# Layer 1's first product in the standard form, weight tile by weight tile over resident tokens

## The chip, the cores and the metric

The program runs on one core of one Trainium2 chip. The core has engines that work side by side, each through its own list of instructions in order: TensorE (PE, matmuls and their weight loads, PEld), VectorE (DVE), ScalarE (ACT) and GpSimd (POOL); SyncE (SP) issues most of the transfers, and ACT and POOL issue some. Instructions wait for one another through semaphores. Data lie in SBUF (128 partitions), matmul results in PSUM, the rest in the chip's memory (DRAM here). The metric is the device time in microseconds (us) of one execution; lower is better.

## The reference

Attention with a bias from relative positions, then two layers of the same kind: a matrix product to 2048 features, an elementwise activation, and a product back to 512. What matters of it:

```python
# q, k, v: (4, 8, 576, 64); x after attention: 2304 tokens x 512
scores = scale * np.matmul(q, k.transpose(0, 1, 3, 2))
scores = scores + bias.transpose(2, 0, 1)[None, :, :, :]
attn = softmax(scores)              # exp(scores - max) / (sum + 1e-09)
x = (attn @ v) as (2304, 512)
h = x @ w_in0                       # layer 0: 512 x 2048
x = (h * np.cos(h)) @ w_out0        # 2048 x 512
h = x @ w_in1                       # layer 1
g = np.maximum(h, 0.0) + alpha * np.minimum(h, 0.0)   # alpha: one number per feature
out = g @ w_out1
```

The inputs come as 64-bit floats. The kernel makes 32-bit floats of them on the chip.

## The kernel before

**Numbers.** Every 64-bit weight tile of 128 x 512 (a *raw*, 512 KB) is read as two 32-bit halves and put together: `conv`, lines 195 to 226, with two ACT steps (L204, L205), two DVE steps (L208 or, with a change of sign, L210; then L212) and a POOL addition (L215). A matmul runs on numbers of reduced precision, so each operand is kept as a rounded part *hi* and a remainder *lo* (`split_to`: ACT makes hi at L234, POOL or DVE the lo at L236), and a product is three matmuls: hi·hi, hi·lo and lo·hi.

**Stages**, one after the other on PE:
1. *Attention*: 16 pairs of heads. Beside it runs a list of background jobs (`JOBS`): the weights of layer 0's first product (`wi0`, 16 tiles; the first `NDIR` = 8 stay in SBUF, the others go to DRAM and come back), and the output weights of layer 0 (`stage_wo(0, k)`, k from 4 to 7; there are 8 sets in all, each from two raws).
2. *Layer 0, first product* (`h_phase0`): 5 token tiles (three of 464, two of 456) x 16 weight tiles x 12 matmuls, standard form (L755). x is fetched and split (L741, L743) for each token tile. The activation h·cos h is ACT L764, DVE L765 and L766, ACT L768, DVE L769, and a write to DRAM (L770). In the background: `stage_wo(0, 0..3)`, kept in SBUF, then sets of layer 1 (`stage_wo(1, k)`, written to DRAM as `w2_d`).
3. *Layer 0, output product* (`o_phase(0)`): a Strassen-Winograd form, 7 products for each of 3 token groups s, 48 matmuls of 384 columns each (L952). The order of the products is `ORD` = 1, 5, 6, 3, 7, 2, 4. Operands (`op`) are fetched, combined (L892) and split (ACT L934, DVE L935). The weight sets `W1[p]` are loaded by SP while the stage begins.
4. *Layer 1, first product* (`h_phase1`): also Strassen-Winograd, 7 products x 8 chunks j x 3 token groups, each 6 matmuls of 384 columns (L1093). `x_prep` makes the combinations of x for each token group (L1065, L234, L236). `chunk_wi1(j)` makes a chunk of weights from two raws with a change of sign by `fl`, which is read from an extra input `alphab` (L298, L300), four sums (L308 to L312) and a split of seven slices (L314 to L316). The activation takes one ACT and one DVE step for each result (L1101, L1102) and a write (L1103).
5. *Layer 1, output product* (`o_phase(1)`): as stage 3, 7 x 3 products, each 72 matmuls of 256 columns. All seven sets of weights are loaded from `w2_d`, 1 MB at a time, two loads a set.

**What sets the order.** Each engine's list of instructions is laid out when the program is built, by a scheduler that places them by the time it reckons for each; the background jobs are generators that the main loops advance by a quota per step (`step`, WR = 2.4 in stage 3). Transfers through `fetch` (L176) go through SP's queue in the order of its list; before, POOL's queue carries ten loads in stage 2 and the writes of L253.

## Time and profile before

| what | us |
|---|---|
| median of 2 runs (lowest, highest) | 1236.49 (1234.80, 1238.19) |
| the profiled execution | 1240.88 |
| its span in the profile | 1238.9 |
| PE busy | 1088.2 (88% of the span), 7120 matmuls |
| PE weight loads busy | 934.3 (75%) |
| DVE busy | 919.1 (74%) |
| ACT busy | 685.2 (55%) |
| POOL busy | 392.0 (32%) |

The profile gives, for each instruction, its start and length on its engine. A *stretch* is a window of time with the busy time of each engine in it. A *timeline* row is a run of like instructions: its start, the length from the first's start to the last's end, and in brackets the idle time before it with what ended that. A *group* adds up the like instructions of a window. Matmuls overlap, so the time of one is the distance between starts and not its own length. The granted clock is the share of TensorE's full clock.

### The profile page before, as it was taken

How to read it: one execution, taken by the hardware profiler on the slowest of the kernel's cores; microseconds unless marked ns; L12 is line 12 of the kernel's file. 1: busy time of each engine (PE TensorE's matmuls, PEld its weight loads, DVE VectorE, ACT ScalarE, POOL GpSimd, SP SyncE). 2: the span in 40 equal slices, each digit the busy share in tenths (PEclk: the TensorE clock that was granted, in tenths of full speed). 3: DMA queues.
4: the chain of work that ended last, by engine and by line, in shares of the span. 5: the costliest groups of instructions: out<-in, count | busy, mean ns of one | idle time of the engine just before them, and what ended most of it. 6: DMA issues, size and time to landing. Idle time of an engine off the chain costs nothing. (4 is left out here: it accounts for less than half of the span.)

```text
span 1238.9 us, 19848 instructions
## 1 busy us (share of the span) xinstructions
PE 1088.2 (88%) x7120; PEld 934.3 (75%) x7120; DVE 919.1 (74%) x1552; ACT 685.2 (55%) x1241; POOL 392.0 (32%) x368
## 2 busy tenths in 40 slices
PE   7598989999878889999699999527999997799998
PEld 2245666666557778899699999527898997799998
DVE  8585777777766999999776767697688644658573
ACT  7595677666765767666544444433455432344442
POOL 6305576554446545433210000362354200000000
PEclk9698999999998999999799999858999998799999
DMA  7566547465457557666858253423365239963631
GB/s 231 185 184 194 180 129 255 168 200 171 157 174 280 175 179 236 221 211 232 306 185 280 64 191 107 162 72 102 128 216 183 106 134 408 347 190 118 211 96 52
DMA packets 117778, 229.80 MB, mean 185 GB/s; under 512 B 13488, under 2 KB 82096, under 8 KB 114992
## 3 DMA queue, kind: packets, MB, share of 16 engines
...
q0 software_dynamic: 5776, 19.93, 4.4%
...
## 5 line engine op out<-in xcount | busy, mean ns | idle before, releaser
L755 PE MATMUL h<-xhi,w 128*128 128x464 f32 (+1 forms) x640 | 191.7, 380 | 17.0 <-DVE tb L769 10.8
L755 PEld LDWEIGHTS h<-xhi,w 128*128 128x128 f32 x640 | 123.2, 193 | 34.4 <-DVE tb L769 13.1
L934 ACT ACTIVATE op<-a 128x768 fp32r<-128x768 f32 x84 | 70.8, 847 | 98.1 <-PE ob L952 26.0
L485 ACT ACTIVATE P<-P,nm 128x576 f32<-128x576 f32 x128 | 98.4, 770 | 47.4 <-DVE nm L472 47.1
L935 DVE TENSOR_TENSOR op<-a,op 128x768 fp32r<-128x768 f32 x84 | 79.5, 956 | 60.2 <-ACT op L934 58.6
L755 PE MATMUL h<-xlo,w 128*128 128x464 f32 (+1 forms) x320 | 120.9, 378 | 0.0
L472 DVE CUSTOM_DVE_ANT_0 P<-S,bt 128x576 f32<-128x576 f32 x128 | 91.8, 751 | 34.0 <-PE S L456 24.5
L215 POOL TENSOR_TENSOR wc<-wc,wp 128x512 int32<-128x512 int32 x64 | 87.4, 1366 | 87.6 <-DVE wc L212 58.3
L934 ACT ACTIVATE op<-b 128x768 fp32r<-128x768 f32 x84 | 70.3, 844 | 71.6 <-PE ob L952 22.5
L935 DVE TENSOR_TENSOR op<-b,op 128x768 fp32r<-128x768 f32 x84 | 80.7, 973 | 33.5 <-ACT op L934 33.5
L1093 PE MATMUL B<-x_t,ch 128*128 128x384 f32 x432 | 88.1, 348 | 10.7 <-DVE g L1158 6.6
L1093 PEld LDWEIGHTS B<-x_t,ch 128*128 128x128 f32 x432 | 78.1, 195 | 15.4 <-DVE g L1158 9.0
L952 PE MATMUL ob<-op,wo 128*128 128x384 f32 x432 | 79.0, 342 | 2.3 <-DVE op L935 2.3
L952 PEld LDWEIGHTS ob<-op,wo 128*128 128x128 f32 x432 | 77.3, 191 | 2.7 <-DVE op L935 2.6
L952 PE MATMUL ob<-wo,op 128*128 128x256 f32 x648 | 78.1, 281 | 0.0
L952 PEld LDWEIGHTS ob<-wo,op 128*128 128x128 f32 x648 | 77.3, 188 | 0.0
L1093 PE MATMUL A<-x_b,ch 128*128 128x384 f32 x288 | 58.7, 351 | 20.6 <-ACT ch L234 11.9
L768 ACT ACTIVATE tb<-tb,hpi 128x464 f32<-128x464 f32 (+1 forms) x80 | 54.1, 677 | 35.0 <-DVE tb L766 34.5
L456 PE MATMUL S<-kh,qh 64*128 64x288 f32 (+1 forms) x288 | 57.1, 352 | 16.4 <-DVE nm L472 16.4
L1093 PEld LDWEIGHTS A<-x_b,ch 128*128 128x128 f32 x288 | 53.0, 198 | 22.9 <-ACT ch L234 12.7
L766 DVE SCALAR_TENSOR_TENSOR tb<-ta,tb 128x464 f32<-128x464 int32 (+1 forms) x80 | 68.5, 859 | 0.7
L952 PE MATMUL oc<-wo,op 128*128 128x256 f32 x432 | 56.5, 293 | 12.4 <-ACT op L934 8.9
...
## 6 DMA issues: line engine op xcount, KB each, us to landing
...
raw<-in_wi_dram SPq DMA_DIRECT2D x32, 512.0 KB, 4.1
raw<-in_wo_dram SPq DMA_DIRECT2D x32, 512.0 KB, 3.9
...
```

The lines of the kernel that those rows point to most:

```text
L215: ge.tensor_tensor(out=c, in0=c, in1=p, op=ALU.add)
L456: te.matmul(ps[:, hf, 0:HS], lhsT=w[r, 128 * i:128 * i + 128], rhs=m[r, c0:c0 + HS], start=(j == 0), stop=(j == 2))
L472: keep(2, ve.tensor_tensor_reduce(out=sn.rearrange("p (a b) -> p a b", a=2), in0=ps[:, :, 0:HS], in1=bt[hp, s].rearrange("p (a b) -> p a b ...
L485: keep(3, se.activation(out=e, in_=e, func=AF.Exp, bias=nm, scale=-1.0, accum_out=sums[n, u][:, col, 0:1]))
L755: te.matmul(ps[:, 0:n], lhsT=w_[:, wx, w], rhs=xx[:, 0:n], start=(j == 0), stop=(j == 11))
L766: ve.scalar_tensor_tensor(out=g, in0=tt, scalar=-C2, in1=g, op0=ALU.mult, op1=ALU.add)
L768: se.activation(out=g, in_=g, func=AF.Sin, bias=hpi)
L934: se.activation(out=o[:, 0], in_=x, func=AF.Copy)
L935: ve.tensor_tensor(out=o[:, 1], in0=x, in1=o[:, 0].bitcast(F32), op=ALU.subtract)
L952: ins = te.matmul(ps[:, m], lhsT=x[:, sl] if L else w[:, sl], rhs=w if L else x, start=first, stop=kk == NK - 1 and n == 2, skip_group_che ...
L1093: ins = te.matmul(ps, lhsT=w[:, wl, sl, 128 * ks:128 * ks + 128], rhs=x[:, xl, ks], start=first and n == 0, stop=n == 5, skip_group_check= ...
```

## The change

Layer 1's first product is now in the standard form. All six token tiles of 384 (`X[q, i]`, hi and lo only) lie in SBUF, and the program goes weight tile by weight tile (f = 0 to 15) over the six: 16 x 6 x 12 = 1152 matmuls of 384 columns instead of 1008. A weight tile `v` comes from one raw (`wi(1, f)`), with hi from ACT and lo from DVE, and there are four buffers for them. The activation is one ACT step (scaled by the sign) and one DVE step (`act2`), and 96 writes to DRAM as before. `alphab`, its loads and the chunk's sums and slices are gone.

The output weights of layer 1 are all made in the background of this stage, k = 0 to 7 with the weight tiles between them. Products 1, 5, 6, 2 and 3 are combined straight into SBUF (`WO[1, g]`, tiles `wq`), and only 7 and 4 pass through DRAM (tiles `wp`). In `o_phase(0)` nothing runs in the background any more.

In layer 0 two sets more (k = 2, 3) are made during attention and only k = 0, 1 in stage 2; `NDIR` is 6; the first x tile is split during attention (pool `xh0`); remainders in `split_to` and those of later x tiles are made on DVE from stage 2 on; and ten weight loads stand on SP's queue instead of POOL's.

The diff, cut to its core:

```diff
-FIRST, SIDE, SMOD, BFIRST, BRATE, SPL, WS0, WSR, PER = 4, 6, 2, 8, 1.75, 3, 30, 3.8, 1.0
+FIRST, SIDE, SMOD, BFIRST, BRATE, SPL, WS0, WSR, PER = 4, 6, 2, 8, 1.75, 3, 28, 3.2, 1.0
...
-NDIR = 8
+NDIR = 6
 XA, HX = 6, 300
 RING, LO = 4, 3
-NW1, WR = 7, 2.4
+NIP, H0R, H1R = 2, 1.0, 3.2
 ORD = (1, 5, 6, 3, 7, 2, 4)
-GRP = ((1,), (5, 6), (3, 7), (2, 4))
+GRPS = (((1,), (5, 6), (3, 7), (2, 4)), ((1,), (5, 6), (2, 3), (7, 4)))
...
+    def leave_w(layer, k, g, x):
+        ps = GRPS[layer][g]
+        n = len(ps)
+        if (layer == 0 and k < NIP) or (layer == 1 and g < 3):
+            w = WO[layer, g]
+            yield from split_to(w[:, :, k, 0, :], w[:, :, k, 1, :], x)
             return
-        st = wpool["t"].tile([128, 2, 2, 256], F32R, tag="st", name=f"sw{layer}_{k}_{places[0][0]}")
...
+        st = wpool["t"].tile([128, 2, 2, 256], F32R, tag="st", name=f"sw{layer}_{k}_{g}")
...
+            order = (cols(u1, 1), ct[:, 0:2], cols(box[1], 2), ct[:, 2:4])
+        for g, x in enumerate(order):
+            yield from leave_w(layer, k, g, x)
-    def chunk_wi1(j):
...
+    def wi(layer, f):
         box = []
-        fl = wpool["f"].tile([128, 256], F32, tag="fl", name=f"fl{j}")
...
+        yield from conv(layer, f, 0, box)
+        if layer:
+            t = wt[f] = wpool["h"].tile([128, 2, 512], F32R, tag="w", name=f"v{f}")
+        elif f < NDIR:
             t = wt[f] = wpool["a"].tile([128, 2, 512], F32R, tag="w", name=f"w{f}")
         else:
             t = wpool["t"].tile([128, 2, 2, 256], F32R, tag="st", name=f"st{f}").rearrange("p a b c -> p a (b c)")
         hi, lo = t[:, 0], t[:, 1]
-        if HIA == 2:
+        if layer:
+            se.activation(out=hi, in_=box[0], func=AF.Copy)
+        elif HIA == 2:
             keep(0, ge.tensor_copy(out=hi, in_=box[0]))
         else:
             keep(0, se.activation(out=hi, in_=box[0], func=AF.Copy))
         yield
-        keep(1, (ge if LOP else ve).tensor_tensor(out=lo, in0=box[0], in1=hi.bitcast(F32), op=ALU.subtract))
+        keep(1, (ve if layer else ge).tensor_tensor(out=lo, in0=box[0], in1=hi.bitcast(F32), op=ALU.subtract))
...
-    JOBS += [(stage_wo, (0, k), 3.0, [(0, 2 * k, 1), (0, 2 * k + 1, 1)]) for k in range(4, NK)]
+    JOBS = [(wi, (0, f), 1.0, [(0, f, 0)]) for f in range(NF)]
+    JOBS += [(stage_wo, (0, k), 3.0, [(0, 2 * k, 1), (0, 2 * k + 1, 1)]) for k in range(NIP, NK)]
...
+                        wpool["x"] = astack.enter_context(tc.tile_pool(name="xh0", bufs=NCC, **right))
...
-                eng = ve if t == 0 and cc % 2 else ge
+                eng = ve if t else ge
...
-                ge.dma_start(out=wt[f], in_=w_d[f])
-            bg.extend(stage_wo(0, k) for k in range(4))
+                fetch(wt[f].bitcast(F32), w_d[f])
+            for g, ps in enumerate(GRPS[0]):
+                for i, p in enumerate(ps):
+                    fetch(WO[0, g][:, i, NIP:4].bitcast(F32), w2_d[0][SLOT[p], :, NIP:4])
+                    if p == 1:
+                        fetch(W1[1].bitcast(F32), w2_d[0][SLOT[1], :, 4:8])
+            bg.extend(stage_wo(0, k) for k in range(NIP))
...
-                quota += 1.6
+                quota += H0R
...
+                due = {(0, 5 if p == 7 else 6, 2 * h): [(W1[p][:, 4 * h:4 * h + 4], 4 * h)] for p in (7, 4) for h in range(2)}
+                weight = lambda p, k, x: W1[p][:, k, x] if p in (4, 7) else WO[1, PLACES[1][p][0]][:, PLACES[1][p][1], k, x]
...
-                bg.extend(stage_wo(1, k) for k in range(NW1))
...
     def h_phase1():
...
+        tiles = [(q, i) for q in range(NS3) for i in range(2)]
...
+            def x_prep(q):
+                x = {i: xs[q].tile([128, 2, NCC, TS], F32R, tag=f"x{i}", name=f"x{q}_{i}") for i in range(2)}
+                for i in range(2):
+                    fetch(x[i][:, 1].bitcast(F32), x1_d[q][:, :, i].rearrange("c p n -> p c n"))
                 yield
-
...
+                for i in range(2):
+                    for h in (slice(0, 2), slice(2, 4)):
+                        yield from split_to(x[i][:, 0, h], x[i][:, 1, h], x[i][:, 1, h].bitcast(F32))
+                    X[q, i] = x[i]
...
-                first = [x_prep(0), chunk_wi1(0), chunk_wi1(1)]
+                first = [x_prep(0), wi(1, 0), x_prep(1), wi(1, 1), wi(1, 2)]
...
+            ph = tile_pool(c, "ph", bufs=6, space=PSUM)
+            bg.append(x_prep(2))
+            nw = 3
+            for k in range(NK):
+                for _ in range(2):
+                    if nw < NF:
+                        bg.append(wi(1, nw))
+                        nw += 1
+                bg.append(stage_wo(1, k))
...
+                for cc in range(NCC):
+                    for wx, xx in ((0, 0), (0, 1), (1, 0)):
+                        ins = te.matmul(ps, lhsT=w[:, wx, 128 * cc:128 * cc + 128], rhs=x[:, xx, cc], start=(n == 0), stop=(n == 11))
...
+            def act2(f, q, i, ps):
+                g = gp.tile([128, TS], F32, tag="g", name=f"u{f}_{q}_{i}")
+                se.activation(out=g, in_=ps, func=AF.Copy, scale=sgn[:, f:f + 1])
+                ve.scalar_tensor_tensor(out=g, in0=ps, scalar=asg[:, f:f + 1], in1=g, op0=ALU.mult, op1=ALU.max)
+                t0 = TS * q + NH * i
+                se.dma_start(out=g_d[1][f, :, t0:t0 + TS], in_=g)
+            quota = 0.0
+            late = None
+            for f in range(NF):
+                for q, i in tiles:
+                    while (q, i) not in X or f not in wt:
+                        step()
+                    ps = emit_h(f, q, i)
+                    if late:
+                        act2(*late)
+                    late = (f, q, i, ps)
+                    quota += H1R
+                    step(int(quota))
+                    quota -= int(quota)
+            act2(*late)
```

The rows below show how the lists of the engines change at three places. In the names, `x1_0` is an x tile (group 1, half 0), `raw1_3_0` the raw of layer 1's weight tile 3, `wc` and `wp` the two halves of a raw in conversion, `v` a weight tile of layer 1, `op2_4_0` an operand of product 4 of token group 2, `o2_4` the last result of layer 0.

**ACT's list where layer 1's first product begins.** Before, from the first operand of layer 0's last product:

```order
L934 ACTIVATE op2_4_0_8483<-b11_2_0_7899 128x768
L934 ACTIVATE op2_4_1_8499<-b11_2_1_7920 128x768
L934 ACTIVATE op2_4_2_8515<-b11_2_2_7943 128x768
L985 ACTIVATE o2_2_8530<-oa2_8061 128x768
L934 ACTIVATE op2_4_3_8534<-b11_2_3_7968 128x768
L960 DMA x1_d2_61<-o2_2_8530 128x2x384
L234 ACTIVATE x_b11_0_8614<-x_b11_0_8614 128x768
L234 ACTIVATE x_b21_0_8615<-x_b21_0_8615 128x768
```

After, from the same operand:

```order
L895 ACTIVATE op2_4_0_8233<-b11_2_0_7748 128x768
L232 ACTIVATE x1_0_8388<-x1_0_8388 128x768 x2
L895 ACTIVATE op2_4_1_8249<-b11_2_1_7766 128x768
L232 ACTIVATE x1_1_8389<-x1_1_8389 128x768 x2
L895 ACTIVATE op2_4_2_8265<-b11_2_2_7784 128x768
L946 ACTIVATE o2_2_8280<-oa2_7878 128x768
L895 ACTIVATE op2_4_3_8284<-b11_2_3_7805 128x768
L921 DMA x1_d2_61<-o2_2_8280 128x2x384
```

Before, from the eviction of the last result (`o2_4`):

```order
L988 ACTIVATE o2_4_8585<-ob2_8140 128x768
L234 ACTIVATE x_b22_0_8616<-x_b22_0_8616 128x768
L960 DMA x1_d2_61<-o2_4_8585 128x2x384
L234 ACTIVATE x_b11_1_8603<-x_b11_1_8603 128x768
L234 ACTIVATE x_t1_0_8617<-xt1_0_8661 128x768
L234 ACTIVATE x_b21_1_8604<-x_b21_1_8604 128x768
L234 ACTIVATE x_t3_0_8618<-xt3_0_8678 128x768
L234 ACTIVATE x_b22_1_8605<-x_b22_1_8605 128x768
L234 ACTIVATE x_t2_0_8619<-xt2_0_8682 128x768
L205 ACTIVATE wp1_1_0_8685<-raw1_1_0_8680 128x512
L234 ACTIVATE ch0_8701<-wc1_0_0_8669 128x512
```

After, up to that eviction and behind it:

```order
L293 ACTIVATE v1_8409<-wc1_1_0_8399 128x512
L206 ACTIVATE wc1_3_0_8525<-raw1_3_0_8523 128x512
L207 ACTIVATE wp1_3_0_8526<-raw1_3_0_8523 128x512
L206 ACTIVATE wc1_2_0_8415<-raw1_2_0_8413 128x512
L206 ACTIVATE wc1_4_0_8571<-raw1_4_0_8569 128x512
L949 ACTIVATE o2_4_8335<-ob2_7945 128x768
L207 ACTIVATE wp1_4_0_8572<-raw1_4_0_8569 128x512
L921 DMA x1_d2_61<-o2_4_8335 128x2x384
L232 ACTIVATE x0_0_8365<-x0_0_8365 128x768 x2
L293 ACTIVATE v2_8422<-wc1_2_0_8415 128x512
L293 ACTIVATE v3_8549<-wc1_3_0_8525 128x512
L232 ACTIVATE x0_1_8366<-x0_1_8366 128x768 x2
```

The splits of six x combinations and a chunk's slices that followed the eviction are gone. Two splits of x tile 1 now stand among the operands of the last product, the hi parts of weight tiles 0 and 1 ahead of the eviction, and one conversion and the splits of x0 behind it.

**SP's list where layer 1's output product begins.** Before (`wo1_p` is half a weight set, `a11_0_0` and the like are parts of the activations):

```order
L176 DMA wo1_1_10660<-w2_d1_78 128x2048
L176 DMA a11_0_0_10711<-g_d1_80 128x2x384
L176 DMA a11_0_1_10713<-g_d1_80 128x2x384
L176 DMA wo1_1_10660<-w2_d1_78 128x2048
L176 DMA a11_0_2_10716<-g_d1_80 128x2x384
L176 DMA a11_0_3_10718<-g_d1_80 128x2x384
L176 DMA wo1_5_10653<-w2_d1_78 128x2048
L176 DMA a22_0_0_10724<-g_d1_80 128x2x384
L176 DMA a21_0_0_10726<-g_d1_80 128x2x384
L176 DMA a22_0_1_10731<-g_d1_80 128x2x384
L176 DMA a21_0_1_10733<-g_d1_80 128x2x384
L176 DMA wo1_5_10653<-w2_d1_78 128x2048
```

After:

```order
L178 DMA a11_0_0_10561<-g_d1_82 128x2x384
L178 DMA a11_0_1_10563<-g_d1_82 128x2x384
L178 DMA a11_0_2_10565<-g_d1_82 128x2x384
L178 DMA a11_0_3_10567<-g_d1_82 128x2x384
L178 DMA wp7_10549<-w2_d1_80 128x2048
L178 DMA a22_0_0_10573<-g_d1_82 128x2x384
L178 DMA a21_0_0_10575<-g_d1_82 128x2x384
L178 DMA a22_0_1_10580<-g_d1_82 128x2x384
L178 DMA a21_0_1_10582<-g_d1_82 128x2x384
L178 DMA wp7_10549<-w2_d1_80 128x2048
L178 DMA a22_0_2_10588<-g_d1_82 128x2x384
L178 DMA a21_0_2_10590<-g_d1_82 128x2x384
```

Of the loads of weight sets, three stood ahead of the eighth load of activations before; now one does, and the four activations of the first product come first.

**PE's list where layer 0's first product begins.** Before:

```order
L755 MATMUL h0_0_4898<-xhi0_0_4870,w0_1666 128x464
L755 MATMUL h0_1_4918<-xhi0_0_4870,w1_1734 128x464
L755 MATMUL h0_2_4945<-xhi0_0_4870,w2_1825 128x464
L755 MATMUL h0_3_4967<-xhi0_0_4870,w3_1961 128x464
L755 MATMUL h0_4_4994<-xhi0_0_4870,w4_2061 128x464
L755 MATMUL h0_5_5018<-xhi0_0_4870,w5_2151 128x464
L755 MATMUL h0_0_4898<-xlo0_0_4862,w0_1666 128x464
L755 MATMUL h0_0_4898<-xhi0_0_4870,w0_1666 128x464
L755 MATMUL h0_0_4898<-xhi0_1_4873,w0_1666 128x464
```

After:

```order
L725 MATMUL h0_0_5002<-xhi0_0_4962,w0_1588 128x464
L725 MATMUL h0_0_5002<-xlo0_0_4954,w0_1588 128x464
L725 MATMUL h0_0_5002<-xhi0_0_4962,w0_1588 128x464
L725 MATMUL h0_0_5002<-xhi0_1_4965,w0_1588 128x464
L725 MATMUL h0_0_5002<-xlo0_1_4956,w0_1588 128x464
L725 MATMUL h0_0_5002<-xhi0_1_4965,w0_1588 128x464
L725 MATMUL h0_0_5002<-xhi0_2_4968,w0_1588 128x464
L725 MATMUL h0_0_5002<-xlo0_2_4958,w0_1588 128x464
```

Before, six weight tiles' first matmuls on one x part stood ahead of the rest; after, the twelve matmuls of weight tile 0 stand in a row.

## Rows read from the trace of the kernel before

**Rows 1.** stretches: length, busy us of each engine, granted clock, DMA share, GB/s
```profile
0.00:375.00 375.00, 321.10 (x2633) 202.86 (x2633) 270.23 (x677) 258.46 (x574) 182.62 (x192) 0.96 0.60 188
375.00:390.00 15.00, 15.00 (x60) 12.93 (x61) 7.86 (x9) 7.82 (x14) 9.24 (x8) 0.83 1.07 389
390.00:594.00 204.00, 193.16 (x903) 171.32 (x902) 195.21 (x315) 140.77 (x240) 93.94 (x92) 0.98 0.59 201
594.00:790.00 196.00, 182.71 (x1009) 180.52 (x1007) 136.55 (x163) 90.00 (x116) 15.57 (x19) 0.96 0.55 182
...
801.00:825.00 24.00, 4.17 (x11) 2.73 (x10) 24.00 (x20) 9.75 (x14) 17.38 (x9) 0.50 0.38 123
825.00:900.00 75.00, 59.07 (x300) 56.46 (x300) 56.80 (x74) 32.01 (x60) 28.90 (x18) 0.87 0.31 104
900.00:1000.00 100.00, 94.22 (x519) 90.68 (x518) 75.75 (x123) 48.17 (x96) 37.80 (x32) 0.98 0.51 166
...
1037.00:1239.00 202.00, 184.80 (x1515) 183.70 (x1513) 125.29 (x139) 80.39 (x98) 0.00 (x0) 0.96 0.56 188
```

**Rows 2.** the same view, 20 us of attention and of layer 0's first product
```profile
240.00:260.00 20.00, 19.61 (x161) 13.17 (x162) 15.49 (x37) 12.75 (x31) 11.01 (x13) 1.00 0.55 186
...
430.00:450.00 20.00, 14.05 (x60) 11.77 (x59) 19.93 (x29) 13.45 (x25) 11.77 (x10) 0.91 0.59 208
```

**Rows 3.** PE's timeline, layer 0's first product: start, length, operation, [idle before]
```profile
374.92 2.69 PE L755 MATMUL h<-xhi,w 128*128 128x464 f32 x6 [6.18 <-ACT xhi L741]
...
395.90 0.59 PE L755 MATMUL h<-xhi,w 128*128 128x464 f32 x2
...
402.88 0.58 PE L755 MATMUL h<-xhi,w 128*128 128x464 f32 x2
```

**Rows 4.** PE's waits from 375 to 594: who waits for whom, us, times, longest
```profile
PE h L755 <- DVE tb L769: 10.8, 5, 4.2
```

**Rows 5.** PE's timeline, output product of layer 0
```profile
610.43 0.69 PE L952 MATMUL oc<-op,wo 128*128 128x384 f32 x1 [7.95 <-ACT op L934]
...
772.55 8.49 PE L952 MATMUL oa<-op,wo 128*128 128x384 f32 x48
780.88 8.56 PE L952 MATMUL ob<-op,wo 128*128 128x384 f32 x48
```

**Rows 6.** PE's timeline, layer 1's first product
```profile
800.42 1.01 PE L1093 MATMUL A<-x_b,ch 128*128 128x384 f32 x2 [10.98 <-ACT ch L234]
...
917.05 2.24 PE L1093 MATMUL B<-x_t,ch 128*128 128x384 f32 x12
919.13 2.24 PE L1093 MATMUL A<-x_b,ch 128*128 128x384 f32 x12
```

**Rows 7.** PE's and ACT's timelines, layer 1's output product
```profile
1057.90 0.58 PE L952 MATMUL oc<-wo,op 128*128 128x256 f32 x1 [8.91 <-ACT op L934]
...
1089.18 8.68 PE L952 MATMUL ob<-wo,op 128*128 128x256 f32 x72
1097.70 2.53 PE L952 MATMUL oa<-wo,op 128*128 128x256 f32 x20
...
1057.01 0.84 ACT L934 ACTIVATE op<-a 128x768 fp32r<-128x768 f32 x1 [11.97 <-DMA a<-g_d]
```

**Rows 8.** groups by shape from 790 to 1037 (POOL, DVE), from 594 (DVE); DMA issues
```profile
L236 POOL TENSOR_TENSOR ch<-ct,ch 128x1024 fp32r<-128x1024 f32 x8 | 20.0, 2494 | 8.0 <-ACT ch L234 8.0
...
L1102 DVE SCALAR_TENSOR_TENSOR g<-A,alpha,g 128x384 f32<-128x384 f32 x24 | 14.7, 613 | 29.6 <-ACT g L1101 29.6
...
L935 DVE TENSOR_TENSOR op<-b,op 128x768 fp32r<-128x768 f32 x80 | 77.0, 974 | 33.5 <-ACT op L934 33.5
...
raw<-in_wi_dram SPq DMA_DIRECT2D x32, 512.0 KB, 4.1
```

**Rows 9.** DVE's groups by shape from 375 to 594
```profile
L766 DVE SCALAR_TENSOR_TENSOR tb<-ta,tb 128x464 f32<-128x464 int32 x48 | 43.4, 907 | 0.3
...
L743 DVE TENSOR_TENSOR xlo<-xlo,xhi 128x464 fp32r<-128x464 f32 x2 | 1.3, 643 | 11.2 <-ACT xhi L741 11.2
```

335 lines of the change are left out of this document (74 added, 261 removed).

## The prediction

> **What bounds the kernel now.** I read the table by stretches first [rows 1], cut where the stages end, because one share for the whole span would average over five stages. The reader is to see in which of them TensorE (PE) is busy nearly all the time, and in which not. Attention (0 to 375) shows 321.1 of 375, but in its middle PE is at 19.61 of 20 [rows 2], so it is a matmul stage with thin ends. The first product of layer 0 (375 to 594) has 208 of 219, the output product of layer 0 (594 to 790) 183 of 196. Layer 1's first product falls in two: from 900 to 1000 PE is busy for 94 of 100, but from 801 to 825 for 4.17 of 24, while VectorE (DVE) is busy for all 24 and GpSimd (POOL) for 17.38. The last stage (1037 to 1239) has 185 of 202.
>
> Then I read PE's timeline for cadences and gaps. In layer 0's first product 33 matmuls of 464 columns start from 395.90 to 402.88 [rows 3]: 0.2115 us each, and by columns 0.2079 for 456. Waits for the activation's last DVE step add up to 10.8 us [rows 4], and 6.18 stand ahead of the stage [rows 3]. In layer 0's output product 48 matmuls start in 780.88 − 772.55 = 8.33 us, 0.1735 each, and one wait of 7.95 stands near its start [rows 5]. In layer 1's first product 12 matmuls start in 2.08 us (917.05 to 919.13), 0.1733 each, and the first of all waits 10.98, until 800.42 [rows 6]. The last stage does 72 in 8.52 us, 0.1183 each [rows 7].
>
> So each stage has a floor, its matmuls times its cadence, and a loss above it:
> - layer 0, first: 576 × 0.2115 + 384 × 0.2079 = 201.7; it takes 219, after the gap of 6. Loss 17 and 6.
> - layer 0, output: 21 × 48 × 0.1735 = 174.9 against 196. Loss 21.
> - layer 1, first: 1008 × 0.1735 = 174.9 against 248, from 789.4 to 1037. Loss 73, of it 11 before the first matmul, 20 from 801 to 825 and 16 from 825 to 900: some 47 at its start.
> - layer 1, output: 21 × 72 × 0.1183 = 178.9 against 202 up to the end of the span. Loss 23, the last copy and its write among it.
>
> **The change, part by part.**
>
> *Layer 1's first product: 25 more of matmuls, 57 less of waiting.* Sixteen weight tiles × 6 token tiles × 12 = 1152 matmuls replace 1008; the floor is 199.9. What goes is the work in front of them. Before, a product needed a chunk (two converted weight tiles, flipped in sign, four sums, a split of seven slices, of which one of 1024 columns takes POOL 2.49 us [rows 8]) and x combinations: DVE formed four of them for each token group. After, the first group of matmuls needs one weight tile and one x tile without a sum. In the order, the splits of the middle token group and of two weight tiles stand ahead of the last eviction of layer 0. Behind it stand one conversion and two halves of x, on ScalarE no step longer than 0.84 [rows 7], and on DVE remainders of 0.95 [rows 8]: 4 × 0.84 + 0.95, some 4.5 us to the first matmul. The second x tile stands behind two weight tiles and two halves more, 3.4, while 12 matmuls run for 2.1: 1.5 to 3 of waiting. The third group's load follows the last write of layer 0: 0 to 2. The granted clock was 0.50 where PE stood idle [rows 1]: 2 for slow matmuls; and 3 for remainders that run beside POOL. Together 11 to 14, and 2 or 3 for the rest of the stage. I take 216, −32. Bounds: 208 (−40), if x is ready in time, and 230 (−18), if two thirds of the hole of 47 stay.
>
> Can weights keep up with 72 matmuls, 12.5 us a tile? Two raw tiles are wanted in that time, and there are two buffers: each has 12.5 us for a load of 4.1 [rows 8] and three reads of less than 0.95. That fits if the reads come without waiting long. DVE's eviction is one step of 0.61 for a token tile [rows 8], 3.7 of 12.5. So neither bounds the stage.
>
> *Layer 0's first product: −19.* The gap of 6 goes, since the first token tile is split during attention; the order has the twelve matmuls of the first weight tile in a row. DVE was the limit early on: 19.93 of 20 from 430 to 450, with PE at 14.05 [rows 2]. From its work here go two of four sets of layer 0's output weights and most of seven sets of layer 1's, with their POOL remainders; 16 remainders of x at 0.64 come to DVE [rows 9], 10 us. The middle activation step, 0.907 on average [rows 9], has less POOL work beside it; near the 0.64 of the other row it would give back 48 × 0.27 = 13. I take the floor 201.7, 2.5 for the clock at the start (0.83 of 15 us [rows 1]) and 2 of stalls: 206 against 225. Bounds −23 (no stall, no slow start) and −10 (the waits of 10.8 stay).
>
> *Attention: +3.* Two more sets of output weights are made here. A set is two conversions and four splits. By half of POOL's 2.49 for 512 columns, six steps a set, that is 15 us of POOL; by 0.84, eight steps, 13 of ScalarE; by 0.95 for full width, some 10 of DVE. They enter a stage where these engines have 192, 117 and 105 us free [rows 1], beside a PE at 19.61 of 20 [rows 2]. No row prices how far they delay the softmax. From below −2 (less of it stands at the stage's end), from above +10 (all of DVE's part). I take 3, nearer to nothing because all three have room; without that room it is the 10.
>
> *Layer 0's output: −2.* Its background work goes, which is little: DVE is idle for 30% here [rows 1]. The wait of 7.95 [rows 5] hangs on loads behind a weight tile in SyncE's (SP's) queue, and in the order a weight load still stands ahead of the same four. New on ScalarE: splits of x tiles stand between the last product's operands, and their loads wait for the product before the last but one, so they start near 773 and are wanted near 783; at two of 0.8 MB, by the 4.1 us of half a megabyte [rows 8] about 6.5 us each, they may be late by some us. Bounds −10 and +4.
>
> *Layer 1's output: −8.* Five of its seven weight sets lie in place; SP carries 4 loads of 1 MB instead of 14. The operand that PE awaited for 8.91 us at 1057.90 had itself waited 11.97 for such an a load [rows 7]. I keep 1 or 2 of that. Bounds −14 (most stalls of the 23) and −2 (the first loads still wait for the last activations).
>
> Moved at no cost: ten weight loads from POOL's queue to SP's during layer 0 (cover: the first six weight tiles, 6 × 2.5 us; without it one landing, 4). The flip input and its DVE steps vanish.
>
> Sum: 3 − 19 − 2 − 32 − 8 = −58. The profiled execution took 1240.9 around its span of 1238.9; that gives 1182.9. It stood 4.4 above the median of the runs, 1236.5, so **1178**.
>
> **A rule against it.** From 900 to 1000 PE's weight loads are busy for 90.68 of 100 [rows 1], and matmuls are what is added. The Trainium skill, "Perfetto Trace Analysis", section "Identifying the Most-Contended Engine", says to find the engine with the highest occupancy, to judge TensorE by the busy share of its weight loads, and to optimise that engine first. By that rule 14% more matmuls make the stage longer, as the first rival has it. The trace agrees for 900 to 1037, and not for 801 to 825, where the weight loads are idle too (2.73 of 24).
>
> **Rivals.**
> - *The matmuls are paid and the hole stays.* x is still split behind the last output of layer 0, at the head of a stage whose floor is 25 higher: 248 + 25 = 273, sum 3 − 19 − 2 + 25 − 8 = −1, about 1235. For it: the x of the third token group can't be read earlier. Against it: the hole was chunk and sum work, which is gone. 4%.
> - *Weights starve the stage.* If reads of the raw tiles queue behind activations that wait for PE, a weight tile takes 14.5 us in place of 12.5: 16 × 14.5 + 13 = 245, sum −29, 1207. For it: ScalarE works in order, and two buffers serve 32 loads. 12%.
> - *The same, further on: slower.* The other terms give −26; slower by 2% (25 us) needs 248 + 51 = 299, 18 us a tile, so waits of 11 us in each buffer's turn beside the load and the reads. 1261. Against it: neither ScalarE nor DVE was full even at 900 to 1000 (48 and 76 of 100). 3%.
> - *Stalls only move.* Attention +8, layer 0 −10 and +2, layer 1 −22 and −2: −24, 1212. 13%.
> - *All cover works.* 0 − 23 − 10 − 40 − 14 = −87: 1150. 10%.
>
> **How the numbers follow.** The forecast has the other 58%, and its own range is 1163 to 1195. The range 1155 to 1210 leaves out the better half of "all cover", the hole and slower cases, and half of "stalls only move": 5 + 4 + 3 + 7 = 19%. Two per cent, about what a measurement of this kernel can tell from no change, lies at 1212 and 1261. Faster: 58 + 10 + 12 + 4 of the 13 = 84%; within: the other 9 and the 4 of the hole, 13%; slower 3%.
>
> **What would show it.** Right: layer 1's first matmul some 5 us after layer 0's last, and from the eighth token tile on 12 matmuls in 2.1 us; no gap over 1 us in layer 0's first product; 206, 216 and 194 us from stage to stage for the terms −19, −32 and −8, and attention's end within 372. Wrong: PE waits for weight tiles at a regular 14 us or more (starvation), or for x at each of the first six token tiles (the hole), or in layer 0's last product for an operand queued behind the splits of x.

## The result, and the profile after

The changed kernel takes 1163.71 us (median of 2 runs, 1161.11 to 1166.31), against 1236.49 before: 0.941 of it, 95% interval 0.931 to 0.952. In a later comparison (e_control below) five runs gave a median of 1165.24, 0.940 of before (0.937 to 0.942). That is 73 us less where 58 were forecast. The profiled execution has a span of 1164.5 in place of 1238.9. In rows, ACTq and SPq stand for the transfers that ACT and SP issue.

The stretches of the kernel after, cut where its stages end (length, busy us of PE, PEld, DVE, ACT and POOL with their instructions, granted clock, DMA share, GB/s):

```profile
0.00:372.00 372.00, 324.03 (x2631) 205.92 (x2632) 267.80 (x677) 257.85 (x572) 178.42 (x182) 0.95 0.59 187
372.00:390.00 18.00, 18.00 (x87) 15.99 (x86) 7.26 (x12) 6.78 (x10) 1.48 (x2) 1.00 1.03 408
390.00:581.50 191.50, 185.58 (x878) 163.79 (x877) 165.19 (x287) 119.87 (x206) 24.80 (x19) 1.00 0.53 183
581.50:761.40 179.90, 176.17 (x1009) 174.56 (x1007) 131.50 (x150) 85.22 (x107) 2.59 (x2) 1.00 0.56 186
761.40:775.00 13.60, 9.65 (x40) 8.96 (x40) 10.51 (x16) 11.50 (x19) 2.86 (x3) 0.75 0.76 237
775.00:900.00 125.00, 125.00 (x723) 125.00 (x722) 89.56 (x153) 71.99 (x131) 32.30 (x30) 1.00 0.61 197
...
968.10:1000.00 31.90, 23.79 (x172) 22.36 (x172) 22.34 (x26) 12.47 (x16) 0.00 (x0) 0.95 0.87 317
1000.00:1164.50 164.50, 159.87 (x1343) 159.67 (x1341) 103.87 (x114) 69.34 (x85) 0.00 (x0) 1.00 0.43 135
```

Set beside [rows 1], layer 1's first product no longer has its stretch of 24 us with PE at 4: it loses 4 us in its first 13.6, at a clock of 0.75, and then PE is busy without a gap to its end, with DVE and ACT at 72% and 58% of the stretch shown. In the first product of layer 0, DVE has 165 of 191.5 where it had 195 of 204, and POOL 25 in place of 94. PE's timeline of the kernel after shows the ends of the stages and the waits at their start:

```profile
372.07 0.61 PE L725 MATMUL h<-xhi,w 128*128 128x464 f32 x1
...
581.48 8.49 PE L913 MATMUL oa<-op,wo 128*128 128x384 f32 x48
590.15 0.44 PE L913 MATMUL oc<-op,wo 128*128 128x384 f32 x1 [0.18 <-ACT op L895]
...
752.92 8.52 PE L913 MATMUL ob<-op,wo 128*128 128x384 f32 x48
763.62 0.45 PE L1017 MATMUL v<-x,v 128*128 128x384 f32 x1 [2.19 <-ACT x L232]
765.04 0.69 PE L1017 MATMUL v<-x,v 128*128 128x384 f32 x1 [0.98 <-DVE x L234]
...
970.69 0.39 PE L913 MATMUL oa<-wq,op 128*128 128x256 f32 x1 [2.57 <-ACT op L895]
```

The waits that were 6.18, 7.95 and 10.98 [rows 3, 5, 6] are now nothing, 0.18 and 2.19. The 10.8 us of waits for the activation in layer 0's first product [rows 4] are 5.9:

```profile
PE h L725 <- DVE tb L739: 5.9, 7, 1.7
```

From such timelines this table is read for every run of the study. A stage ends with its last matmul, or where the first matmul of the next stage starts, if that comes sooner. Attention begins at the span's start, and the last stage ends with the span.

| run | span | attention | layer 0, first | layer 0, output | layer 1, first | layer 1, output |
|---|---|---|---|---|---|---|
| before | 1238.9 | 368.7 | 225.1 | 195.6 | 248.1 | 201.4 |
| after | 1164.5 | 372.1 | 209.4 | 180.0 | 206.7 | 196.4 |
| after, e_control | 1162.2 | 371.7 | 207.2 | 179.7 | 207.4 | 196.3 |
| e_bg | 1186.1 | 372.3 | 209.7 | 196.6 | 209.6 | 197.9 |
| b_nw0 (of before) | 1300.1 | 371.3 | 219.7 | 182.1 | 309.2 | 217.8 |
| e_m1008 | 1139.4 | 371.7 | 209.0 | 179.6 | 181.9 | 197.2 |
| e_l0old | 1177.2 | 364.7 | 227.4 | 181.9 | 206.4 | 196.8 |
| e_nip4 | 1178.1 | 374.2 | 218.0 | 181.2 | 207.1 | 197.6 |
| e_x0late | 1185.6 | 369.9 | 231.1 | 181.6 | 206.6 | 196.4 |
| e_pool | 1172.9 | 370.7 | 214.7 | 179.6 | 211.0 | 196.9 |
| e_wodram | 1188.3 | 373.6 | 206.9 | 182.1 | 207.4 | 218.3 |
| e_x2first | 1166.9 | 371.3 | 209.1 | 179.7 | 211.3 | 195.5 |
| e_raw1 | 1171.1 | 367.6 | 208.5 | 182.1 | 215.9 | 197.0 |
| e_best2 | 1159.1 | 372.3 | 208.8 | 180.5 | 205.8 | 191.6 |

Before to after, the five stages give +3.3, −15.7, −15.6, −41.4 and −5.0: −74.4. The prediction had +3, −19, −2, −32 and −8.

### The profile page after: what moved, and what is told of

Same layout as the page of the kernel before. It is cut to its first block, busy times and chain, and to the rows that moved or that the text cites. A ratio compares the mean times of both kernels' runs of the same rounds, so it can differ in the third digit from the quotient of the medians.

```text
span 1164.5 us, 19858 instructions
## 1 busy us (share of the span) xinstructions
PE 1090.2 (94%) x7264; PEld 944.0 (81%) x7264; DVE 837.8 (72%) x1500; ACT 666.6 (57%) x1200; POOL 254.1 (22%) x248
## 4 chain that ended last, share of the span: by engine, by line
PE 71%; DMA 11%; DVE 7%; ACT 5%; issue 2%; POOL 2%; SPq 0%; ACTq 0%; DVEq 0%; POOLq 0%
PE v L1017 17%; PE ob L913 13%; PE h L725 11%; PE oc L913 7%; PE oa L913 7%; PE S L423 4%; DMA w_d<-sw 3%; PE x_B L540 3%; ACT P L452 2%; PE T_A L505 2%; PE T_B L505 1%; PE x_A L540 1%; DMA rk<-in_k_dram 1%; DMA bias_d<-be 1%; PE bps L135 1%
## 5 line engine op out<-in xcount | busy, mean ns | idle before, releaser
L1017 PE MATMUL v<-x,v 128*128 128x384 f32 x1152 | 202.7, 337 | 3.9 <-ACT x L232 2.2
L1017 PEld LDWEIGHTS v<-x,v 128*128 128x128 f32 x1152 | 201.8, 189 | 4.9 <-ACT x L232 2.5
L725 PE MATMUL h<-xhi,w 128*128 128x464 f32 (+1 forms) x640 | 188.3, 373 | 5.9 <-DVE tb L739 5.9
L216 POOL TENSOR_TENSOR wc<-wc,wp 128x512 int32<-128x512 int32 x64 | 84.1, 1315 | 455.3 <-DMA x_d<-o 265.4
L1025 ACT ACTIVATE u<-v,sgn 128x384 f32<-128x384 f32 x96 | 55.4, 577 | 67.8 <-PE v L1017 59.9
L1026 DVE SCALAR_TENSOR_TENSOR u<-v,asg,u 128x384 f32<-128x384 f32 x96 | 58.8, 613 | 47.0 <-ACT u L1025 46.2
L734 ACT ACTIVATE ta<-h,quart 128x464 int32<-128x464 f32 (+1 forms) x80 | 50.9, 636 | 40.8 <-PE h L725 18.1
L735 DVE SCALAR_TENSOR_TENSOR tb<-ta,h 128x464 f32<-128x464 int32 (+1 forms) x80 | 50.1, 627 | 25.7 <-ACT ta L734 24.8
L725 PEld LDWEIGHTS h<-xlo,w 128*128 128x128 f32 x320 | 60.1, 188 | 6.7
L423 PEld LDWEIGHTS S<-kh,qh 64*128 64x128 f32 (+1 forms) x288 | 31.6, 193 | 35.5 <-DVE nm L439 12.7
```

The costliest lines, as they stand in the source:

```text
L216: ge.tensor_tensor(out=c, in0=c, in1=p, op=ALU.add)
L423: te.matmul(ps[:, hf, 0:HS], lhsT=w[r, 128 * i:128 * i + 128], rhs=m[r, c0:c0 + HS], start=(j == 0), stop=(j == 2))
L725: te.matmul(ps[:, 0:n], lhsT=w_[:, wx, w], rhs=xx[:, 0:n], start=(j == 0), stop=(j == 11))
L1017: ins = te.matmul(ps, lhsT=w[:, wx, 128 * cc:128 * cc + 128], rhs=x[:, xx, cc], start=(n == 0), stop=(n == 11))
L1025: se.activation(out=g, in_=ps, func=AF.Copy, scale=sgn[:, f:f + 1])
L1026: ve.scalar_tensor_tensor(out=g, in0=ps, scalar=asg[:, f:f + 1], in1=g, op0=ALU.mult, op1=ALU.max)
```

## The experiments

Two terms were far off: the output product of layer 0 gave 16 us where 2 were forecast, and layer 1's first product 9 more. There were two theories on the first. By the *backlog theory* the background work on layer 1's sets (the output weights that the kernel before made in layer 0) held DVE and ACT up in the stage ahead, so that the last activations came late. By the *queue theory* a weight load ahead of the loads of activations in SP's queue held them up. Every edit is of the changed kernel, unless it says otherwise, and the edits are cut to their core.

**Layer 1's sets back in layer 0 (e_bg).**

```diff
+            if L == 0:
+                bg.extend(stage_wo(1, k) for k in range(7))
...
+                if L == 0 and i >= 8:
+                    quota += 2.4
+                    step(int(quota))
+                    quota -= int(quota)
```

> The changed kernel, with seven sets of layer 1's output weights made once more in the background of layer 0's first and output products, as the kernel before made them there; they are written to a DRAM tile that nothing reads, and the sets that count are made in layer 1 as in the changed kernel. Backlog theory (the wait of 8 us at the start of layer 0's output product came from DVE work in the stage ahead of it, which made the last activations late): DVE gets some 7 x 6 = 42 us more and is full again; layer 0's first product goes from 209 to 215 to 225, its last activation ends 6 us or more behind the last matmul in place of 4, and the output product waits 5 us or more at its start: 180 becomes 187 to 196. Queue theory (the wait came from the weight load ahead of the loads of activations in SP's queue, and something else in the change took it away): output product stays at 180 to 183. Layer 1's stages stay at 207 and 196 by both.

The output product of layer 0 goes from 180 to 196.6, about the length that it had before. The first product ahead of it, where half of the sets' splits run (14 of 28), stays at 209.7; the 215 to 225 expected there did not come. So the sets lengthen the stage behind. Rows of PE, ACT and SP of this run, at the end of layer 0's first product (its last matmul ends at 582.2):

```profile
600.53 0.69 PE L914 MATMUL oc<-op,wo 128*128 128x384 f32 x1 [9.99 <-ACT op L896]
```

```profile
591.93 0.63 ACT L233 ACTIVATE sw<-wc 128x512 fp32r<-128x512 f32 x1 [3.73 <-DMA w_s<-sw]
591.95 0.33 ACTq L741 DMA_DIRECT2D g_d<-tb  x1
```

```profile
582.73 0.72 SPq L179 DMA_DIRECT2D raw<-in_wo_dram  x1
593.99 2.08 SPq L179 DMA_DIRECT2D b<-g_d  x4
```

The last activation's write is issued at 591.95, ten us after the last matmul. Its last DVE step ends at 588.85, some 7 us behind PE; the other 3 come because the write stands in ACT's list behind a split of a set, and that split waits 3.73 us for the one staging tile (`sw`) to be written out. The loads of activations that need this write go out at 593.99, and PE waits 10 us for what they bring.

The kernel before loses its time in the same place, but not at the last write. The last row of the first block tells who waited for whom from 560 to 597, in all, how often, and the longest time:

```profile
593.64 0.34 SPq L176 DMA_DIRECT2D raw<-in_wi_dram  x1
594.16 0.76 SPq L176 DMA_DIRECT2D wo<-w_d  x1
595.01 4.00 SPq L176 DMA_DIRECT2D b<-g_d  x4
SPq L176 <- DVE wc L212: 40.5, 3, 16.2
```

```profile
603.91 0.63 DVE L765 SCALAR_TENSOR_TENSOR tb<-ta,h 128x456 f32<-128x456 int32 x1 [3.74 <-DMA g_d<-tb]
607.82 0.75 DVE L240 SCALAR_TENSOR_TENSOR sw<-wc,sgn,sw 128x512 fp32r<-128x512 f32 x1 [1.24 <-ACT sw L238]
608.49 0.95 DVE L892 TENSOR_TENSOR b<-b,b 128x768 f32<-128x768 f32 x1
```

There the last matmul ends at 594.0. In SP's list a raw stands ahead of the weight load and the four loads of activations (`b`). The raw needs a buffer that DVE's conversion of a set (L212) still reads, and SP waits for it for 16.2 us, until 593.6. Then all these loads go out together, while the DMA engines are 98% busy from 593.85 to 610.43, and those of `b` take 10.0 to 11.2 us to land. At DVE their first sum (L892, 608.49) stands behind the last activations, one of which had waited 3.74 us for a tile, and behind the remainder of a set. Only then comes the operand that PE awaits for 7.95 us. So the queue had a part in it, but what held it was a raw behind DVE's work on the sets, not the weight load.

After the change no set stands there. The four loads go out from 582.10 on, 0.6 us after the last matmul, and land in 6.1 to 8.5 us, which the first product's 8.5 us all but cover. The last write goes out at 585.56, four us behind PE:

```profile
584.89 0.63 DVE L739 TENSOR_TENSOR tb<-h,tb 128x456 f32<-128x456 f32 x1 [0.74 <-ACT tb L738]
```

```profile
585.56 0.33 ACTq L740 DMA_DIRECT2D g_d<-tb  x1
```

**The kernel before without those sets in layer 0 (b_nw0).**

```diff
-NW1, WR = 7, 2.4
+NW1, WR = 0, 2.4
...
-                if j >= 3 and NW1 + j - 3 < NK:
-                    side.append(stage_wo(1, NW1 + j - 3))
+                side.append(stage_wo(1, j - 2))
+                if j >= 6:
+                    side.append(stage_wo(1, j))
```

> The kernel before, with all eight sets of layer 1's output weights made in layer 1's first product and none in layer 0. Backlog theory: layer 0's first product falls from 219 to 205 to 213 and its output product from 196 to 178 to 186, since DVE then follows the matmuls; layer 1's first product grows from 248 to 260 or more. Queue theory: the output product stays at 193 to 197, with a wait of 6 to 8 us at its second product.

The other way round, with the same answer: 195.6 becomes 182.1, though the weight load still stands ahead of the same four loads of activations. The wait of 7.95 is gone; one of 2.7 stays. SP of this run, whose last matmul of the first product ends at 591.1:

```profile
578.76 0.33 SPq L176 DMA_DIRECT2D wo<-w_d  x1
579.19 11.51 SPq L176 DMA_DIRECT2D b<-g_d  x4
```

With no raw of a set in the way, these loads go out one by one as the activations are written, and all four are out when the output product begins. So a weight load ahead in the queue is not the cause, in either kernel; the sets are, by the two ways shown. What the backlog theory said of the first product was mostly wrong: without the sets it takes 219.7 in place of 225.1, where 205 to 213 were expected, so some 18 of its 23 us above the floor (the gap of 6 with them) are layer 0's own. The sets then starve layer 1 (309 us, and a wait of 31 at the head of the last stage): the form before could not have taken them there, at least in this order.

**The price of the form (e_m1008).** 144 matmuls are left out, so that 1008 stay; the sums lack those parts.

```diff
-                n = 0
+                n, last = 0, 10 + f % 2
...
+                        if n == last:
+                            continue
```

> The changed kernel with 1008 matmuls in layer 1's first product in place of 1152: of each token tile's twelve the last one or two are left out, so the sums lack one or two of their twelve parts. It prices the form itself. If that stage is bound by matmuls alone: 144 x 0.1735 = 25 us less in that stage (207 to 182) and in the time. If the weight chain or the activations stand close behind the matmuls: 10 to 18 less, with waits for weight tiles.

The median falls to 1139.85 (0.919 of before, 0.917 to 0.922), the stage from 206.7 to 181.9: 24.8 for 144 matmuls, 0.172 each. The added matmuls are paid in full, as the first expectation said, and PE waits for no weight tile but the first: nothing stands close behind them.

**Layer 0's part undone (e_l0old).** Four sets in its first product, eight weight tiles resident, the first x tile split after attention, remainders of layer 0 on POOL, weight loads on POOL's queue; layer 1's sets stay where the change put them.

```diff
-NIP, H0R, H1R = 2, 1.0, 3.2
+NIP, H0R, H1R = 4, 1.6, 3.2
...
-NDIR = 6
+NDIR = 8
...
-                xp = xh_p if t else wpool["x"]
+                xp = xh_p
...
-                eng = ve if t else ge
+                eng = ve if t == 0 and cc % 2 else ge
...
-                fetch(wt[f].bitcast(F32), w_d[f])
+                ge.dma_start(out=wt[f], in_=w_d[f])
```

> The changed kernel with its layer 0 part undone, but for the sets of layer 1's output weights, which stay in layer 1: four sets of layer 0's output weights in its first product, eight weight tiles resident, the first token tile split after attention, remainders of layer 0 on POOL, ten weight loads less two on POOL's queue, the old constants of the background. Sum of the prediction for these: attention -3, gap +6, layer 0's first product +5 to +10, output product 0 to +4: 8 to 17 us slower than the changed kernel. If the layer 0 part is worth nothing by itself (all of its gain is the moved sets): within 4 us.

1178.89 (0.950 of before, 0.947 to 0.954): 14 to 15 us over the changed kernel, inside the expected 8 to 17. The first product takes 227.4 with the old rows back, a gap of 7.06 and 11.0 us of waits for the activation; the output product stays short at 181.9. So layer 0's part, with the sets of layer 1 already gone, is worth 14 or 15 of the 73.

**Its pieces (e_nip4, e_x0late, e_pool).** First the sets 2 and 3 alone:

```diff
-NIP, H0R, H1R = 2, 1.0, 3.2
+NIP, H0R, H1R = 4, 1.6, 3.2
```

with the background's start and rate as before (30, 3.8).

> The changed kernel with sets 2 and 3 of layer 0's output weights back in its first product (none of them through DRAM), with the old constants for the start and rate of the background. By the prediction's step for attention: attention ends 2 to 4 us earlier (369 in place of 372), and layer 0's first product pays it back with DVE work in its first 60 us: 4 to 8 us more (209 to 213 to 217), time 0 to 5 us over the changed kernel. If two sets among attention cost more than that step says: attention ends 5 us or more earlier and the time falls or stays.

1177.15 (0.950, 0.947 to 0.952), 12 to 13 over the changed kernel in place of 0 to 5. Layer 0's first product pays 8.6, a little more than expected (11.5 us of waits for the activation in place of 5.9), and attention gives nothing back: it ends at 374.2. Over the eleven runs whose program has two sets more or the first x tile in attention, or both, its end lies between 367.6 and 374.2, and over the three with the old load at 364.7, 368.7 and 371.3, so these profiles can't tell the loads apart.

Nor did the two sets run there. The changed kernel has 13 of the 32 splits of layer 0's output weights in attention, the kernel before 16. These are ACT's splits of them from 372 to 582 in the changed kernel, 19 in all:

```profile
L232 ACT ACTIVATE sw<-wt 128x512 fp32r<-128x512 f32 x6 | 3.8, 625 | 4.8 <-DMA w_d<-sw 4.8
L232 ACT ACTIVATE sw<-wc 128x512 fp32r<-128x512 f32 (+1 forms) x5 | 2.7, 539 | 0.2
L232 ACT ACTIVATE wo<-wt 128x512 fp32r<-128x512 f32 x4 | 2.5, 627 | 0.9 <-DVE wt L259 0.9
L232 ACT ACTIVATE wo<-wc 128x256 fp32r<-128x256 f32 (+1 forms) x4 | 2.1, 514 | 0.0
```

So the work that the program gives to attention is not done when attention ends, and e_nip4, with 17 of these splits in layer 0's first product, has no more of them there than the changed kernel. It does it sooner (the last at 449 in place of 479), and with the remainders of 15 splits on DVE in place of 8, since those that go to DRAM (`sw`) keep theirs on POOL. Which of the two costs the 8.6 was not told apart.

The split of the first x tile:

```diff
-                xp = xh_p if t else wpool["x"]
+                xp = xh_p
```

> The changed kernel with the first token tile of layer 0 split after attention, as before. By the prediction: the gap of 6 to 7 us between attention's last matmul and layer 0's first comes back and nothing else moves, 1170 in place of 1164. Rival: the gap only uncovers what the first activations wait for anyway (they fall behind early in that stage), so the stage gives back 3 us or more of it, and the time is within 3 us of the changed kernel.

1189.52 (0.962, 0.957 to 0.967): 24 to 26 us worse, and neither theory had it. The gap is 23.69, not 6 or 7:

```profile
393.62 2.69 PE L724 MATMUL h<-xhi,w 128*128 128x464 f32 x6 [23.69 <-ACT xhi L710]
```

```profile
373.35 7.90 SPq L178 DMA_DIRECT2D w<-w_d  x8
...
384.66 8.00 SPq L178 DMA_DIRECT2D xlo<-x_d  x8
```

With all loads on SP's queue, the loads of x go out behind ten weight loads; from 369 to 394 the DMA engines are full at 407 GB/s. In the kernel before, POOL's queue issued the weight loads, x left SP's at 369.77, and the gap was 6.18 [rows 3]; e_l0old, which has that again, shows 7.06. So the move of weight loads to SP's queue, costed at nothing with some 4 us if its cover failed, costs about 17 without the cover, and the early split is that cover. That is a comparison with e_l0old and the kernel before, which differ in more than the queue; no run moved the loads alone.

The remainders back on POOL:

```diff
-                eng = ve if t else ge
+                eng = ve if t == 0 and cc % 2 else ge
...
-        (eng or (ve if pinned else ge)).tensor_tensor(out=lo, in0=w, in1=hi.bitcast(F32), op=ALU.subtract)
+        (eng or ge).tensor_tensor(out=lo, in0=w, in1=hi.bitcast(F32), op=ALU.subtract)
```

> The changed kernel with the remainders of x in layer 0's first product, of the output weights and of layer 1's x back on POOL. If POOL beside DVE stretches the activation's middle step, as the prediction took it for 13 us of DVE: that step's mean goes from 0.71 to 0.85 or more, layer 0's first product from 209 to 212 to 218. If DVE's 15 us of remainders weigh more than that: the stage stays at 209 or falls. Layer 1's first matmuls wait for remainders of 2 us and more in place of 0.95: 2 to 6 us more there.

5.3 us more in layer 0's first product, 4.3 in layer 1's, as expected (a single run of 1174.64). In the latter a remainder on POOL is what PE waits for; in the former the activation's middle step grows, though less than expected (0.71 to 0.85 or more), and whether that makes the 5.3 is not shown:

```profile
PE v L1017 <- POOL x L234: 4.2, 2, 4.0
```

```profile
L736 DVE SCALAR_TENSOR_TENSOR tb<-ta,tb 128x464 f32<-128x464 int32 x48 | 38.7, 812 | 0.2
```

against 764 ns in the changed kernel and 907 before [rows 9]:

```profile
L736 DVE SCALAR_TENSOR_TENSOR tb<-ta,tb 128x464 f32<-128x464 int32 x48 | 36.5, 764 | 0.4
L739 DVE TENSOR_TENSOR tb<-h,tb 128x464 f32<-128x464 f32 x48 | 30.3, 632 | 8.3 <-ACT tb L738 8.2
L735 DVE SCALAR_TENSOR_TENSOR tb<-ta,h 128x464 f32<-128x464 int32 x48 | 30.1, 627 | 10.4 <-ACT ta L734 9.5 <-DMA g_d<-tb 0.6 <-ACT wo L232 0.2
```

**All sets of layer 1 through DRAM (e_wodram).**

```diff
-        if (layer == 0 and k < NIP) or (layer == 1 and g < 3):
+        if layer == 0 and k < NIP:
...
+                for p in (1, 5, 6, 2, 3):
+                    g, i = PLACES[1][p]
+                    for h in range(2):
+                        due.setdefault((0, p, 2 * h), []).insert(0, (WO[1, g][:, i, 4 * h:4 * h + 4], 4 * h, p))
```

> The changed kernel with all seven products' sets of layer 1 written to DRAM in its first product and loaded when its output product begins, 14 loads of 1 MB in place of 4; 40 more writes on POOL's queue. By the prediction (loads of weights push back loads of activations): 6 to 10 us more in the output product (196 to 202 to 206), nothing in the first product. If what that stage waits for is the last activations alone: within 2 us.

21.9 us more in the last stage, where 6 to 10 were expected (a single run of 1190.14). The first matmul waits 18.05:

```profile
988.04 0.58 PE L917 MATMUL oa<-wq,op 128*128 128x256 f32 x1 [18.05 <-ACT op L899]
```

```profile
986.63 0.63 ACT L232 ACTIVATE sw<-wt 128x512 fp32r<-128x512 f32 x1 [4.71 <-DMA w_d<-sw]
987.17 3.03 ACT L899 ACTIVATE op<-a 128x768 fp32r<-128x768 f32 x4
```

The first operand stands in ACT's list behind the last splits of the sets, and the last three of these wait 2.0, 4.8 and 4.7 us for their one staging tile, as in e_bg. Loads on SP's queue are late too in this run, and how much they add was not told apart. In this order, sets made this late cost 22 us if they go through DRAM; that most of them stay in SBUF is what lets them leave layer 0.

**Where layer 1's first product starts (e_x2first, e_raw1).** First another order of the token groups:

```diff
-        tiles = [(q, i) for q in range(NS3) for i in range(2)]
+        tiles = [(q, i) for q in (2, 0, 1) for i in range(2)]
```

> The changed kernel with the third token group first in layer 1's first product, which can be read only once layer 0's last result is written. If the choice of the first group is what keeps the start short: the first matmul comes 10 to 14 us after layer 0's last in place of 2, and the stage takes 214 to 218 in place of 207. If the start is set by work on DVE and ScalarE, as in the kernel before: within 3 us of 207, since that work is the same.

```profile
769.25 0.69 PE L1017 MATMUL v<-x,v 128*128 128x384 f32 x1 [9.21 <-ACT x L232]
```

The first matmul waits 9.2 in place of 2.2, somewhat less than expected, and the stage takes 211.3, 4 to 5 more. The write and the load of the last token group together are no longer than that, so the start has no hole like the one of before in any of the three orders tried (e_best2 has the third); the first group's being ready is worth 4.

Then one raw buffer for two:

```diff
-            wpool["s"] = tile_pool(c, "ws", bufs=2, **right)
+            wpool["s"] = tile_pool(c, "ws", bufs=1, **right)
```

> The changed kernel with one buffer in place of two for raw tiles in layer 1's first product. It prices the rival of starved weights: a raw's turn is then a load of 4.1 us, three reads and their waits, some 7 us, and two are wanted for each weight tile: 14 us in place of 12.5, so the stage takes 225 to 235 in place of 207, with waits for weight tiles. If reads wait long behind activations (turns of 9 us): 250 or more. If the sets of output weights only end later: within 5 us of 207, and the output product pays.

215.9, 8.5 to 9 us more and not 18 to 28, and PE waits mostly for DVE's evictions, 9.2 us in nine waits, not for weight tiles:

```profile
PE v L1017 <- DVE u L1026: 9.2, 9, 1.6
```

A conversion that waits for its raw tile stands ahead of the next evictions in ACT's list:

```profile
875.41 0.67 ACT L206 ACTIVATE wc<-raw 128x512 f32<-128x512 f32 x1 [2.36 <-DMA raw<-in_wi_dram]
```

Even with half the buffers no starvation of weight tiles comes: the rival of 12% had little ground.

**Two orders changed (e_best2).** The middle token group, whose splits are done first, goes first; the weight sets 7 and 4 are loaded one product later, behind the loads of activations.

```diff
-        tiles = [(q, i) for q in range(NS3) for i in range(2)]
+        tiles = [(q, i) for q in (1, 0, 2) for i in range(2)]
...
-                first = [x_prep(0), wi(1, 0), x_prep(1), wi(1, 1), wi(1, 2)]
+                first = [x_prep(1), wi(1, 0), x_prep(0), wi(1, 1), wi(1, 2)]
...
-                due = {(0, 5 if p == 7 else 6, 2 * h): [(W1[p][:, 4 * h:4 * h + 4], 4 * h)] for p in (7, 4) for h in range(2)}
+                due = {(0, 6 if p == 7 else 7, 2 * h): [(W1[p][:, 4 * h:4 * h + 4], 4 * h)] for p in (7, 4) for h in range(2)}
```

> The changed kernel with two orders changed: layer 1's first product takes the middle token group first, whose tiles are split before layer 0's last product ends (and weight tile 0 before it too), then the first and the third; and the two weight sets that come from DRAM (7 and 4) are loaded one product later in layer 1's output product, behind the loads of activations. If the 4 us at the start of layer 1's first product are the splits of the first group alone: they fall below 1 us. If the 8 us at the start of the output product come from weight loads ahead of activations in SP's queue: 3 to 5 of them go. Together 1156 to 1160. If the last activations set that start instead: its 8 us stay and only 3 to 4 are won.

The control beside it, the changed kernel unedited:

> The changed kernel itself, on the chip of the runs beside it: 1160 to 1167, with layer 1's first product at 207 and its output product at 196, so that stage lengths can be compared within one chip.

1154.92 (0.932 of before, 0.929 to 0.935) against 1165.24 for the control (0.940, 0.937 to 0.942). That is 0.9% less: four of its five runs lie below all five of the control, and the fifth, 1161.13, just above the control's lowest, 1160.76. The two stages whose order was changed give 6.3 of the 10 us. The output product gains 4.7 as expected:

```profile
970.03 0.39 PE L913 MATMUL oa<-wq,op 128*128 128x256 f32 x1 [2.57 <-ACT op L895]
...
980.99 2.39 PE L913 MATMUL oc<-wq,op 128*128 128x256 f32 x19
```

its first wait stays, and of the waits of its second product, 5.0 us in the control, 1.3 are left. Layer 1's first product starts at once, but gains only 1.6, since its third group is reached sooner and now waits 3.1:

```profile
761.69 6.58 PE L1017 MATMUL v<-x,v 128*128 128x384 f32 x37
...
772.69 0.44 PE L1017 MATMUL v<-x,v 128*128 128x384 f32 x1 [1.52 <-ACT x L232]
774.71 5.54 PE L1017 MATMUL v<-x,v 128*128 128x384 f32 x23 [1.58 <-DVE x L234]
```

The other 4 us of the medians' difference the profiles don't show: the profiled execution of e_best2 is its slowest run, and its span is only 3.1 shorter than the control's, since the stages ahead take 3 us more.

## Why the prediction was right, and where it was off

The forecast was 1178 with a range of 1155 to 1210, and the likeliest case's own range began at 1163; the time is 1163.7, at its edge. The direction and the main mechanism held: matmuls were added at full price, and the starved start in front of them went. Two of the terms came out near for other reasons than those given. The terms:

- *Layer 1's first product*, −32 forecast, −41.4 measured, just beyond the bound of −40. The floor was right (1152 × 0.1735 = 199.9, and e_m1008 gives 0.172 each). Mis-sized was the loss at the start, taken as 11 to 14 and measured at 6.8 (206.7 − 199.9): 4.0 of waits and about 3 of slow matmuls at a clock of 0.75 for 13.6 us. The prediction added the four steps on ACT one after the other (4.5 to the first matmul; it was 2.2, since the matmul starts on the first half of x) and then 1.5 to 3 for the second tile and up to 2 for the third group, which both came in time. It summed what runs side by side.
- *Layer 0's output product*, −2 forecast, −15.6 measured, beyond the bound of −10. This is the step that failed. It read the wait of 7.95 [rows 5] as hanging on a weight load in SP's queue, saw that load still in the order, and left the wait in place. e_bg and b_nw0 show that the sets of layer 1 caused it: in the kernel before by a raw that held SP's queue for 16.2 us behind DVE's conversions, and by their place ahead of the first sum at DVE; in e_bg by way of the last activations' writes. The prediction counted only the background work within this stage, "which is little", and took DVE's full load in the stage ahead [rows 2, 430 to 450] for a limit of that stage alone. What counts is the end of that stage, where DVE is busy for 23.0 of the 24 us from 570 to 594, and without the sets, in b_nw0, for 17.3 of the last 21. The stall feared there from x splits among the last operands did not come: behind one of 1.93 at 605, no wait stands until 761.
- *Layer 0's first product*, −19 forecast, −15.7 measured. The gap went and the clock was at 1.00 at once. But of the reasons given for a lighter DVE, two of four sets gone did not hold: 19 splits of layer 0's sets run here, against 16 before. The sets of layer 1, which did go, are worth 5.4 in the kernel before (b_nw0) and 0.3 in the changed one (e_bg); layer 0's own part 18 (e_l0old), of which the gap is 7. Waits of 5.9 stayed where 2 were allowed, 3.5 of them from 402 to 423 (DVE is busy for 8.0 of 8 us from 402 to 410 and for 18.8 of the next 20), the rest from 477 to 492. That "no gap over 1 us" would be seen was wrong: three waits are longer, up to 1.67.
- *Attention*, +3 forecast, +3.3 measured: the agreement is luck. The two sets that it priced did not run there (13 splits against 16), and attention's end lies anywhere from 364.7 to 374.2 in these runs.
- *Layer 1's output product*, −8 forecast, −5.0 measured. Of 4 loads on SP's queue one still stood ahead of the second product's activations; e_best2 moves it and gets 4.7.
- *Moved at no cost*: the cover was not the first weight tiles but the early split of x; without it, about 17 us by e_x0late.

Of the rivals, "all cover works" (1150) came nearest from the other side: its −40 for layer 1's first product and −10 for layer 0's output were surpassed, while attention, layer 0's first product and the last stage gave less. "The matmuls are paid and the hole stays" was right in its price, not in its hole. The Trainium skill, "Perfetto Trace Analysis", section "Identifying the Most-Contended Engine", calls the engine with the highest occupancy the most contended and says to optimise it first. By that rule 144 more matmuls lengthen the stage, and e_m1008 measures just that, 24.8; the stage got shorter all the same because the engine stood idle for more than that at its start. The rule holds for each stretch, and here for all but the first 14 us of the stage.

The contention of DVE and POOL, which the prediction took from the stretched middle step of the activation, is borne out: that step reads two tiles in SBUF and takes 0.907 on average before, 0.812 with the remainders back on POOL and 0.764 after, while the step before it, with one input in PSUM, takes 0.626, 0.631 and 0.627. Step by step it is plainer: where no instruction of POOL overlaps the middle step, it takes 0.63 in both kernels (42 steps before, 65 after); where one does, it takes 1.15 on average before (34 steps) and 1.08 after (14), by POOL's spans, which the profile gives only roughly. The Trainium skill, "SBUF — State Buffer", section "Who interferes with whom", says that a DVE instruction with two SBUF inputs contends with a GpSimd instruction that reads SBUF, and that one with at most one SBUF input does not, outside the modes in which DVE uses both its ports; these rows agree.
